# Regrouping the input loads of a one-token attention and GLU kernel: one load for wq, four heads of K per load, V in four, two, one and one heads

## The chip, the cores and the metric

The kernel runs on one core of a Trainium2 chip. The core has a matrix engine (TensorE, PE in the profile, with its weight loads as PEld), a vector engine (VectorE, DVE), a scalar engine (ScalarE, ACT), GpSimd (POOL) and SyncE (SP), which here only issues data transfers. Sixteen DMA engines move data between the off-chip memory and the on-chip memory. The metric is the device time of one execution in microseconds. Before the change it is 82.23 us, the median of five runs (82.16 to 82.81).

## The reference

One token `x` (512 values) goes through two branches, and a sigmoid gate mixes them. Branch A is attention over the last 4096 positions of a cache with 8 key/value heads and 32 query heads of 128 values. Branch B is a gated linear unit of width 1792.

```python
W = min(4096, max(256, Sk // 4))                 # 4096
q = (x @ wq) in 32 heads of 128
k = k_cache[:, :, Sk - W:, :]; v = v_cache[:, :, Sk - W:, :]   # each head serves 4 query heads
p = softmax(q @ k^T * Dh ** -0.5)
a = (p @ v) flattened @ wo
b = (sigmoid(x @ w_gate) * (x @ w_up)) @ w_down
g = sigmoid(sum(x * gate_w))
out = g * a + (1 - g) * b
```

All inputs are bfloat16. They come to 30.67 MB: wq and wo 4.19 MB each, the windows of K and V 8.39 MB each, w_gate, w_up and w_down 1.84 MB each. Each byte is used once.

## The kernel before, in words

**Loads.** All large inputs are loaded by one queue, SyncE's (`dq = nc.sync`), in the order of the program: wq in two halves (line 77), K in four loads of two heads (`kn`, line 86 through `load_blocks`, line 80), w_gate and w_up (lines 90 and 92), V in loads of two, two, two and one heads (`vv`, lines 102 and 104), half of w_down (105), V's last head (106), the rest of w_down (107), and wo in six pieces (112). The two short vectors `x` and `gate_w` come through ScalarE's queue (lines 70 and 71).

**Buffers.** K and V share the pool `blk`. It has four buffers, and each holds two heads: for each of the 128 partitions, 32 rows of 128 values of each head, 8 KB per head. V's first four-buffer round therefore goes where K was: the first V load waits until VectorE has read heads 0 and 1 of K, the second until it has read heads 2 and 3, and so on. wo uses wq's buffer (tag `big`). SyncE executes its instructions in order, so all that stands behind a waiting load waits too. A load also waits for the load that used its completion semaphore before, which is about eight loads earlier.

**Query.** TensorE computes q with x's four chunks as the stationary side and wq as the moving side: 32 matmuls of 512 columns in four blocks (line 160). ScalarE copies each block to on-chip memory (162), VectorE transposes it in 32 x 32 blocks (163), and eight small VectorE copies place it in a zeroed selection matrix `qbig` (172).

**Scores.** For each of the eight key heads VectorE transposes the head's K in 32 x 32 blocks of 4-byte elements (`kT`, line 180; four buffers), and eight matmuls accumulate scores for all heads in one PSUM tile (185). VectorE and ScalarE then form the softmax numerators (192 to 205) and VectorE transposes them (`eT`, 207).

**Branch B, values, output.** 32 matmuls make gate and up (215), VectorE and ScalarE the gated product and its transpose (221 to 231). The value matmuls (267) take eight per head and wait for the V load of their head. Heads are handled in two groups of four; each group ends with a ScalarE copy (272), eight small matmuls (277) and a VectorE multiplication (279). After the second group VectorE and TensorE bring the result into columns (283 to 287). `add_row` (248) accumulates w_down's and wo's products in one row: 28 matmuls for w_down and 64 for wo. The result is copied and stored in two halves (294 to 297).

The order on each engine is set by a scheduler of the framework, which moves instructions between the independent chains; the order of the loads on SyncE is the program's.

Of the kernel before, what the change touches and what calls it, by code (L numbers as in the profile page):

```python
# [12 lines left out]
BF16 = mybir.dt.bfloat16  # L13
# [4 lines left out]
def kernel(  # L18
# [16 lines left out]
    P = 128  # L35
    D = A_x.shape[-1]
    DC = D // P
    Hkv = A_k_cache.shape[1]
# [5 lines left out]
    KB = W // P  # L44
# [12 lines left out]

    const = ctx.enter_context(tc.tile_pool(name="const", bufs=1))
    big = ctx.enter_context(tc.tile_pool(name="big", bufs=1))
    blk = ctx.enter_context(tc.tile_pool(name="blk", bufs=4))  # L60
    w14 = ctx.enter_context(tc.tile_pool(name="w14", bufs=3))
    ktp = ctx.enter_context(tc.tile_pool(name="ktp", bufs=4))
    work = ctx.enter_context(tc.tile_pool(name="work", bufs=1))
# [9 lines left out]
    dq = nc.sync  # L73
    wq_sb = big.tile([P, DC, HQ * DH], BF16, name="wq_sb", tag="big")
    wq_v = A_wq.rearrange("(p c) n -> p c n", c=DC)
    for i in range(2):
        dq.dma_start(wq_sb[:, 2 * i:2 * i + 2, :], wq_v[:, 2 * i:2 * i + 2, :])  # L77

    def load_blocks(t, cache, g0, n, at=0):
        dq.dma_start(t[:, at:at + n, :, :],  # L80
                     cache[0, g0:g0 + n, SBASE:SBASE + W, :].rearrange("g (p kb) d -> p g kb d", kb=KB))

    kn = []
    for i in range(Hkv // 2):
        t = blk.tile([P, 2, KB, P], BF16, name="kn", tag="blk")
        load_blocks(t, A_k_cache, 2 * i, 2)
        kn += [t[:, 0], t[:, 1]]

    wg_sb = w14.tile([P, DC, F], BF16, name="wg_sb", tag="w14")
    dq.dma_start(wg_sb[:], B_w_gate.rearrange("(p c) f -> p c f", c=DC))  # L90
# [4 lines left out]
    wd_v = B_w_down.rearrange("(p j) n -> p j n", j=NJ)  # L95

    vv = []
    for i in range(Hkv // 2):
        t = blk.tile([P, 2, KB, P], BF16, name="vv", tag="blk")
        vv += [t[:, 0], t[:, 1]]  # L100
        if i < Hkv // 2 - 1:
            load_blocks(t, A_v_cache, 2 * i, 2)
        else:
            load_blocks(t, A_v_cache, 2 * i, 1)
            dq.dma_start(wd_sb[:, 0:NJ_A, :], wd_v[:, 0:NJ_A, :])
            load_blocks(t, A_v_cache, 2 * i + 1, 1, at=1)
            dq.dma_start(wd_sb[:, NJ_A:NJ, :], wd_v[:, NJ_A:NJ, :])

    wo_sb = big.tile([P, NC_O, N_OUT], BF16, name="wo_sb", tag="big")
# [218 lines left out]
```

## Time and profile before

| | |
|---|---|
| median of 5 runs | 82.23 us |
| profiled execution, its own time | 82.23 us |
| its span, first to last instruction | 80.2 us |
| TensorE busy | 51.2 us, 64% of the span |
| VectorE busy | 35.2 us, 44% |
| ScalarE busy | 9.0 us, 11% |
| queue of the loads | 30.67 MB, its packets fill 92.4% of 16 engines' span |
| transposes of K, line 180 | 8 of 2274 ns |
| score matmuls, line 185 | 64, busy 16.1 us |
| value matmuls, line 267 | 64, busy 12.7 us |

The span is what the profile covers; the time of a run also holds what lies before the first and after the last instruction. Busy time is a union of an engine's instructions. Matmuls are pipelined and overlap, so the mean duration of one is longer than the pace at which they go; where a pace is needed, it is read from a stretch of time and the number of matmuls that it holds. "DMA to landing" is the time from the issue of a load to its completion, with the wait in the queue. In rows by window the columns are the window, its length, busy time and number of instructions of PE, PEld, DVE, ACT and POOL, the granted TensorE clock, the DMA engines' busy share, and GB/s.

### The profile page before, as it was taken

Reading aid. Unit: us, or ns where it says so; the run is one execution under the profiler, and the core shown is the slowest. Engines: PE = TensorE matmul, PEld = TensorE weight load, DVE = VectorE, ACT = ScalarE, POOL = GpSimd, SP = SyncE. Lnnn points to the kernel's source line nnn. Section 1 sums busy time; section 2 is a strip of 40 time slices with the busy share of each in tenths; the row PEclk is TensorE's granted clock in tenths of the full one; section 3 lists DMA queues with packets and bytes.
Section 4 is the critical chain, followed back from the end, with each engine's and each line's share of the span. In section 5 each row is a group of like instructions: output and inputs, shape, how many; then the busy total and the mean of one; then the engine's idle time right before and its main releaser. Section 6 shows DMA issues by size and latency. Waiting matters only on the chain.

```text
span 80.2 us, 777 instructions
## 1 busy us (share of the span) xinstructions
PE 51.2 (64%) x313; PEld 23.2 (29%) x313; DVE 35.2 (44%) x43; ACT 9.0 (11%) x13; POOL 5.0 (6%) x10
## 2 busy tenths in 40 slices
PE   0010995999200499999997475958599656745560
PEld 0000531334000133444442233322533323533330
DVE  0006400052999999999923437999100000200020
ACT  2300000555500000000000080001100002000010
POOL 7970000000000000000000000000000000000000
PEclk9999999999995557999999999999955999999996
DMA  5699999999999999999999999999999999999400
GB/s 99 261 425 417 449 433 384 445 413 437 413 437 404 433 409 430 444 429 436 415 408 425 404 429 417 421 425 417 428 415 440 411 424 403 425 421 396 181 11 1
DMA packets 3930, 30.71 MB, mean 383 GB/s; under 512 B 340, under 2 KB 472, under 8 KB 984
## 3 DMA queue, kind: packets, MB, share of 16 engines
q1 hardware_dynamic: 3922, 30.67, 92.4%
q8 instruction: 2, 0.03, 0.2%
q10 hardware_dynamic: 6, 0.00, 0.0%
HBM read 30.67 MB, written 0.00 MB: 382 GB/s over the span
## 4 chain that ended last, share of the span: by engine, by line
DMA 65%; DVE 15%; PE 9%; issue 6%; ACT 1%; SPq 0%
DMA vv<-in_A_v_cache_dram 27%; DMA wo_sb<-in_A_wo_dram 23%; DMA wq_sb<-in_A_wq_dram 15%; DVE kT L180 11%; PE q_ps L160 7%; DVE qbig L172 2%; DVE qtT L163 2%; PE a_ps L248 2%; ACT q_sb L162 1%; DVE res L294 0%; SPq L77 0%
## 5 line engine op out<-in xcount | busy, mean ns | idle before, releaser
L185 PE MATMUL S_ps<-kT,qbig 128*128 128x512 bf16 x64 | 16.1, 414 | 6.6 <-DVE qbig L172 6.6
L180 DVE STREAM_TRANSPOSE kT<-kn 128x2048 f32<-128x2048 f32 x8 | 17.8, 2274 | 0.0
L267 PE MATMUL pv_ps<-vv,eT 128*16 128x512 bf16 (+1 forms) x64 | 12.7, 435 | 3.0 <-DMA vv<-in_A_v_cache_dram 3.0
L160 PE MATMUL q_ps<-wq_sb,xT 128*128 128x512 bf16 x32 | 11.1, 524 | 0.8 <-DMA wq_sb<-in_A_wq_dram 0.8
L185 PEld LDWEIGHTS <-qbig 128*128 128x128 bf16 x64 | 6.6, 104 | 16.1 <-DVE qbig L172 7.4
L267 PEld LDWEIGHTS <-eT 128*16 128x16 bf16 (+1 forms) x64 | 4.6, 99 | 10.0 <-issue 5.5
L163 DVE STREAM_TRANSPOSE qtT<-q_sb 128x512 f32<-128x512 f32 x4 | 2.8, 700 | 9.0 <-ACT q_sb L162 9.0
L248 PE MATMUL a_ps<-wo_sb,oY 128*1 128x256 bf16 x64 | 4.3, 272 | 3.1 <-DMA wo_sb<-in_A_wo_dram 3.1
L160 PEld LDWEIGHTS <-xT 128*128 128x128 bf16 x32 | 3.9, 126 | 7.5 <-issue 6.2
L279 DVE TENSOR_TENSOR oT<-o_ps,rb 128x16 bf16<-128x16 f32 x2 | 0.3, 175 | 12.4 <-PE o_ps L277 12.4
L162 ACT CAST q_sb<-q_ps 128x1024 bf16<-128x1024 f32 x4 | 4.0, 1012 | 8.7 <-PE q_ps L160 8.7
L248 PEld LDWEIGHTS <-oY 128*1 128x1 bf16 x64 | 2.8, 83 | 4.5 <-issue 3.7
L294 DVE CAST res<-a_ps 1x256 bf16<-1x256 f32 x1 | 0.4, 411 | 7.9 <-PE a_ps L248 7.9
L141 DVE TENSOR_TENSOR gpr<-xr 1x512 f32<-1x512 bf16 x1 | 0.7, 680 | 6.7 <-DMA xr<-in_gate_w_dram 6.7
L133 PE MATMUL xt_ps<-ident,xr 1*128 1x1 bf16 x4 | 0.3, 165 | 5.2 <-POOL ident L118 5.2
L126 POOL MEMSET qbig<- 128x4160 bf16 x1 | 3.6, 3564 | 0.0
L272 ACT COPY pv_sb<-pv_ps 128x512 f32<-128x512 f32 x2 | 1.2, 586 | 18.2 <-PE pv_ps L267 18.2
L277 PE MATMUL o_ps<-identf,pv_sb 128*128 128x16 f32 x16 | 2.1, 265 | 1.4 <-ACT pv_sb L272 1.4
L224 DVE RECIPROCAL sg<-sge 128x448 f32<-128x448 f32 x1 | 3.0, 2954 | 0.0
L202 ACT ACTIVATE nb<-mb_ps 128x1 f32<-128x1 f32 x1 | 0.2, 171 | 24.4 <-PE mb_ps L199 24.4
L277 PEld LDWEIGHTS o_ps<-identf,pv_sb 128*128 128x128 f32 x16 | 1.9, 191 | 2.4 <-ACT pv_sb L272 2.4
L192 DVE TENSOR_REDUCE pm<-S_ps 128x1 f32<-128x1024 f32 x1 | 1.2, 1225 | 2.7 <-PE S_ps L185 2.7
(49 smaller groups left out, 26.0 us busy)
## 6 DMA issues: line engine op xcount, KB each, us to landing
kn<-in_A_k_cache_dram SPq DMA_DIRECT2D x4, 2048.0 KB, 20.8
vv<-in_A_v_cache_dram SPq DMA_DIRECT2D x3, 2048.0 KB, 21.4
wq_sb<-in_A_wq_dram SPq DMA_DIRECT2D x2, 2048.0 KB, 9.6
wo_sb<-in_A_wo_dram SPq DMA_DIRECT2D x3, 1024.0 KB, 24.1
vv<-in_A_v_cache_dram SPq DMA_DIRECT2D x2, 1024.0 KB, 19.7
wg_sb<-in_B_w_gate_dram SPq DMA_DIRECT2D x1, 1792.0 KB
wu_sb<-in_B_w_up_dram SPq DMA_DIRECT2D x1, 1792.0 KB, 32.6
wd_sb<-in_B_w_down_dram SPq DMA_DIRECT2D x2, 896.0 KB, 21.5
```

The costliest lines, as they stand in the source:

```text
L126: nc.gpsimd.memset(qbig[:], 0.0)
L160: nc.tensor.matmul(q_ps[:, hb, :], lhsT=xT[:, c:c + 1].to_broadcast([P, P]), rhs=wq_sb[:, c, n0:n0 + 512], start=(c == 0), stop=(c == DC - 1))
L162: nc.scalar.copy(q_sb[:, k * 1024:(k + 1) * 1024], q_ps[:].rearrange("p a b -> p (a b)"))
L163: nc.vector.transpose(qtT[:].bitcast(F32)[:, k * 512:(k + 1) * 512], q_sb[:].bitcast(F32)[:, k * 512:(k + 1) * 512])
L172: nc.vector.tensor_copy(q_dst[rows, :, 32 * qd:32 * qd + REP, :, t], q_src[rows, :, :, :, 0, t])
L180: nc.vector.transpose(kT[:].bitcast(F32), kn[g].rearrange("p k d -> p (k d)").bitcast(F32))
L185: nc.tensor.matmul(S_ps[:, hb, :], lhsT=q_st[:, g, dhi, :, t], rhs=k_v[:, hb * 16:(hb + 1) * 16, dhi, :, t], start=(g == 0 and dhi == 0 an ...
L192: nc.vector.tensor_reduce(pm[:], S_f, axis=AX.X, op=ALU.max)
L224: nc.vector.reciprocal(sg[:], sge[:])
L248: nc.tensor.matmul(a_ps[32 * i:32 * i + 1, i, 0:HN], lhsT=lhsT, rhs=rhs[:, i * HN:(i + 1) * HN], start=start, stop=stop)
L267: nc.tensor.matmul(pv_ps[32 * gq:32 * gq + mm, :, :], lhsT=eT[:, g, 4 * m:4 * m + wj, :].rearrange("p k h -> p (k h)"), rhs=vv[g][:, 4 * m ...
L277: nc.tensor.matmul(o_ps[:], lhsT=pv_sb[:, j, :], rhs=sel_v[:, j, :, :], start=(j == 0), stop=(j == 3))
```

## The change

The pool `blk` gets two buffers of four heads in place of four buffers of two; the memory is the same. wq is loaded by one transfer. K is loaded by two transfers of four heads. V is loaded by one transfer of four heads into the first buffer, and into the second by transfers of two, one and one heads, with the halves of w_down between as before. Nothing else is edited.

```diff
-    blk = ctx.enter_context(tc.tile_pool(name="blk", bufs=4))
+    blk = ctx.enter_context(tc.tile_pool(name="blk", bufs=2))
...
-    for i in range(2):
-        dq.dma_start(wq_sb[:, 2 * i:2 * i + 2, :], wq_v[:, 2 * i:2 * i + 2, :])
+    dq.dma_start(wq_sb[:], wq_v)
...
-    for i in range(Hkv // 2):
-        t = blk.tile([P, 2, KB, P], BF16, name="kn", tag="blk")
-        load_blocks(t, A_k_cache, 2 * i, 2)
-        kn += [t[:, 0], t[:, 1]]
+    for i in range(2):
+        t = blk.tile([P, 4, KB, P], BF16, name="kn", tag="blk")
+        load_blocks(t, A_k_cache, 4 * i, 4)
+        kn += [t[:, j] for j in range(4)]
...
-    for i in range(Hkv // 2):
-        t = blk.tile([P, 2, KB, P], BF16, name="vv", tag="blk")
-        vv += [t[:, 0], t[:, 1]]
-        if i < Hkv // 2 - 1:
-            load_blocks(t, A_v_cache, 2 * i, 2)
+    for i in range(2):
+        t = blk.tile([P, 4, KB, P], BF16, name="vv", tag="blk")
+        vv += [t[:, j] for j in range(4)]
+        if i == 0:
+            load_blocks(t, A_v_cache, 0, 4)
         else:
-            load_blocks(t, A_v_cache, 2 * i, 1)
+            load_blocks(t, A_v_cache, 4, 2)
+            load_blocks(t, A_v_cache, 6, 1, at=2)
             dq.dma_start(wd_sb[:, 0:NJ_A, :], wd_v[:, 0:NJ_A, :])
-            load_blocks(t, A_v_cache, 2 * i + 1, 1, at=1)
+            load_blocks(t, A_v_cache, 7, 1, at=3)
             dq.dma_start(wd_sb[:, NJ_A:NJ, :], wd_v[:, NJ_A:NJ, :])
```

## The prediction

> **What bounds the kernel now.** I read the page's slices and queues first, then the chain that ended last, then SyncE's own instructions and waits, then the stages of the DMA stream.
>
> ```profile
> DMA  5699999999999999999999999999999999999400
> DMA packets 3930, 30.71 MB, mean 383 GB/s; under 512 B 340, under 2 KB 472, under 8 KB 984
> q1 hardware_dynamic: 3922, 30.67, 92.4%
> q8 instruction: 2, 0.03, 0.2%
> ```
>
> The DMA engines are full from the third slice (4 us) to the thirty-seventh (74 us). 92.4% of 80.2 us is 74.1 us of packets per engine: all 30.67 MB arrive through one queue without a hole. The chain, in order of time, ends so:
>
> ```profile
> 36.28 21.65 DMA vv<-in_A_v_cache_dram
> 57.92 0.02 issue
> 57.94 18.38 DMA wo_sb<-in_A_wo_dram
> 76.32 0.04 issue
> 76.36 1.25 PE a_ps L248 x16
> 77.61 0.40 DVE res L294
> ```
>
> From 36.3 us on the chain is load, load, sixteen matmuls, a copy. All arithmetic before that is behind the stream. So two questions decide: does the change shorten the stream, and does any engine become so late that the stream runs dry, or that work is left over when it ends?
>
> ```profile
> 1.64 2.21 SPq L80 DMA_DIRECT2D kn<-in_A_k_cache_dram  x4
> 25.67 15.34 SPq L80 DMA_DIRECT2D vv<-in_A_v_cache_dram  x4
> SPq L80 <- DVE kT L180: 21.2, 4, 7.6
> L180 DVE STREAM_TRANSPOSE kT<-kn x8: 2268/2268/2312, 20.6 to 38.4; 128x2048 f32<-128x2048 f32 x8
> DMA to landing us min/median/max: 16.3/20.8/25.2
> ```
>
> The first two are SyncE's timeline, the third its waits, the last two the instructions on the tile kn. V loads wait for VectorE's transposes, because they reuse K's buffers; the first is issued at 25.67. K loads landed at 1.64 + 16.3 = 17.9, then about 22.9 (2.11 + 20.8), then 27.95 (2.75 + 25.2): 5.0 us per 2 MB, with no gap between them. The transposes occupy VectorE nearly without a pause from 20.6 to 40.6.
>
> ```profile
> 8.00:13.00 5.00, 4.11 (x10) 1.69 (x11) 0.89 (x6) 0.17 (x1) 0.00 (x0) 1.00 0.99 424
> 14.00:32.00 18.00, 11.36 (x36) 4.09 (x35) 13.40 (x17) 4.05 (x4) 0.00 (x0) 0.81 1.02 425
> 33.00:40.50 7.50, 7.50 (x36) 3.31 (x34) 7.50 (x4) 0.00 (x0) 0.00 (x0) 1.00 1.01 428
> 42.00:57.00 15.00, 10.41 (x81) 4.63 (x80) 9.79 (x11) 2.51 (x5) 0.00 (x0) 1.00 1.01 419
> ```
>
> These are windows (last columns: TensorE clock, DMA share, GB/s): mostly wq, then K, then gate and up, then V. Packets of 16, 8, 14 and 8 KB run at 424, 425, 428 and 419 GB/s: the size of packets above 8 KB hardly matters.
>
> **Part 1, fewer and larger loads.** wq 2 loads become 1, K 4 become 2, V 5 become 4: four fewer. K and V keep their 8 KB packets, since one head's rows for a partition are 8 KB whatever the load holds. Only wq changes packets: a partition's four chunks lie together, so 32 KB in place of 2 x 16 KB. The trace's single packets, by size, have medians of 312 ns (8 KB), 540 (14 KB), 611 (16 KB) and 9 (the 4 B semaphore write that each engine makes per load). The straight line through 8 and 16 KB has 0.0365 ns per byte and 13 ns at zero, so an estimate for 32 KB is 13 + 1196 = 1209 ns. Per engine: wq 16 x 611 = 9.78 becomes 8 x 1209 = 9.67, a gain of 0.10; four semaphore writes 4 x 9 = 0.04. Sum -0.14 us.
>
> No row shows a 32 KB packet. Lower end: -0.10 as worked out. Upper end: the sixteen first packets of wq take 1.2 to 1.7 us, about 0.7 over 0.61; if this start-up grew with the packet, doubling it would add 0.7. Nearer rows deny growth: single 8 KB packets ahead of the kernel exceed their 0.31 by 0.13 to 0.24, the two 16 KB instruction fetches exceed 0.61 by 0.41 in the middle of traffic, so it looks like latency. If packets are cut back to 16 KB, 0. I take -0.10.
>
> **A rule weighed.** The Trainium skill's page "DMA: Bandwidth & Descriptors", section "Anatomy of one DMA — SWDGE (gpsimd) path", gives a DMA about 2.0 us fixed plus bytes / 436e3, measured on the other issue path. Paid in turn, a 2 MB K load would take 2.0 + 4.8 = 6.8 us, and four fewer loads would save 8 us: 74. The row says 5.0 us from landing to landing, which leaves room for 0.2 at most, and most of this is data at 425 GB/s (4.93). The fixed part is hidden under the next load's packets. I take the row: -0.04.
>
> **Part 2, q starts later.** Half of wq let 8 matmuls run in 8.64 to 12.23; the other 24 began at 13.06. Now all 32 begin when wq is whole, about 12.9. Ends of the q blocks, read from where ScalarE's copies start, are 14.94, 16.65, 18.90, 20.62: after the restart, eight matmuls in 3.59 us, eight in 2.25, eight in 1.72. So 32 take 3.59 + 2.25 + 2 x 1.72 = 9.3, to 22.2, 1.6 later. The page "TensorE: Matmul & The Clock Gate", section "Part 1: The HAM clock gate (the "warmup" mystery)", speaks against the change: lost early work is lost warm-up, some 3.4 us at half clock after an idle time. By the rule 8 cold matmuls (3.4) and 24 warm (24 x 0.216 = 5.2) end at 21.5. The row is 0.7 longer; I take it. The granted clock reads 1.00 here, but the 0.45 us per matmul in the row shows the slow start.
>
> **Part 3, K lands in fours.** Heads 0 to 3 now land when heads 2 and 3 did, 22.9 instead of 17.9; heads 4 to 7 at 32.9 as before. VectorE: the last q copy ends at 23.3, its transpose at 24.0, eight selection copies (1.76) at 25.8, then eight transposes at a pitch of 2.21: heads 0 to 3 done at 34.6, the eighth at 43.5, 2.9 later than 40.6. If two transposes go ahead of the copies, as now, the sums stay within 0.5.
>
> Score matmuls: start 28.0. TensorE has then idled 5.8 us, and will start slow as now (10 in 4.26 us at clock 0.54, the other 54 at 0.217 each). That needs 16.0, to 44.0, but the last head can only begin at 43.5: 43.5 + 8 x 0.217 = 45.2, 2.0 later than 43.2. From there to the transposed weights eT it is 5.5 us as now (43.23 to 48.74): 50.7.
>
> **Part 4, V's waits.** The first V load needs heads 0 to 3: issue at 34.6 instead of 25.7. Queued behind it on SyncE are all other V loads, wd and wo, and TensorE and the stream wait for those. The cover is wu: it lands at 8.90 + 32.6 = 41.5, and a first packet starts 1.0 after issue (0.74 to 1.74). The stream runs dry only if that V load is issued after about 40, so 5 us are spare. The second half needs head 7 (43.5); by then the first 4 MB keep the stream busy until about 51, so 7 us are spare. The loads of wd and wo keep their order; their waits on a load some eight earlier end later (wo's third on the first V load, 52.9), with 10 us of data still queued. SyncE's long issue of wg (4.96 us) stays harmless: nothing follows until 34.6. Cost 0.
>
> **Part 5, TensorE catches up.** Heads 0 to 3 start when the 4 MB V load lands, with heads 2 and 3 now: 52.9. 4 x 1.39 = 5.6 to 58.5, copy 0.65, eight small matmuls 1.06: 60.2. Heads 4 to 6 take 4.2 (64.4), half of wd 0.93 (65.3), head 7 1.9 (67.2), against 67.0 now. A stretch at half clock adds about 0.04 per matmul (16 in 3.44 against 16 in 2.78), 0.7 for one stretch. The slack at the end: after the o chain (69.36 now) TensorE needs 0.93 + 4 x 1.04 = 5.1 us, so it could start as late as 77.57 - 5.1 = 72.5: 3.1 us spare. Cost 0; without the cover each us is one us.
>
> **Sum.** 80.21 - 0.14 = 80.07 in the span; the profiled execution took 82.23, the median too, so 2.0 lie around it: **82.1 us**.
>
> **Rivals.**
> - TensorE becomes the bound (slower). Mechanism: half clock lasts through the score matmuls. From eT to the o chain TensorE needs 18.6 us less the wait for V, 16.7 of work, so it decides only when eT is later than 72.5 - 16.7 = 55.8, with half clock (0.427 each) beyond about 46. If it lasted throughout, 28.0 + 27.3 + 5.5 + 16.7 = 77.5, 5.0 past 72.5: up to 87; a typical case 83.5. For it: the record has 0.50 in the stage already. Against: it ended after 6.8 us. 0.06.
> - Start-up grows with wq's packet: 82.1 + 0.7 = 82.8. 0.07.
> - Instruction fetches collide (slower). Among the trace's single packets, the two instruction fetches at 41.90 and 66.35 each leave one engine about 1.5 us behind the other fifteen to the end; they hit different engines, and the last wo load completes on fourteen by 75.7, on two at 77.2. On one engine it would be 83.6. Nothing in the change steers that. 0.04.
> - Larger loads stream better (faster): wq, K and V (20.97 MB) at 428 instead of 421 is 0.8 us: 81.3. Against: 8 KB packets sit at 309 to 314 ns. 0.09.
> - The stream bounds as now: 0.74.
>
> **How the numbers follow.** 0.5% (0.41 us) is what a measurement can tell. Likeliest 82.1. The range 81.75 to 82.8 holds the stream's case and the start-up rival, and leaves out the two other slower ones and most of the faster one (0.18). Faster 0.09, same 0.74, slower 0.06 + 0.07 + 0.04 = 0.17.
>
> **What would show it.** DMA full to about 75 and wo's last landing near 77.1; first V issue near 34.6, ahead of wu's landing; q ending near 22, transposes near 43.5, the first value matmul near 53; 17 loads' worth of semaphore packets. Wrong if the DMA row has a hole near 41, if the last wo matmuls no longer wait for a DMA, or if wq lands past 13.5.

## The result and the profile after

The changed kernel takes 81.94 us, the median of 43 runs (81.64 to 82.34), against 82.20 for the kernel before (80 runs). The ratio of the two is 0.9954, with a 95% interval from 0.9943 to 0.9966. That is 0.26 us by the medians and 0.38 by the ratio, faster by about the 0.5% that was called the limit of what a measurement can tell. The prediction was 82.1 in a range of 81.75 to 82.8, with no change as the likeliest. An execution that took over 1.5% more than the fastest of its kernel counts as slow and is left out of the ratios, which below concerns one of four executions of the kernel with one buffer, four of twelve with 6 more matmuls and two of four with 24.

The page of the changed kernel, slices and queues:

```profile
span 80.1 us, 774 instructions
DMA  6869979999999999999999999999999999999400
DMA packets 3739, 30.71 MB, mean 383 GB/s; under 512 B 277, under 2 KB 409, under 8 KB 921
q1 hardware_dynamic: 3730, 30.67, 92.1%
q8 instruction: 2, 0.03, 0.2%
```

The stream is full as before, to the thirty-seventh slice, with no hole near 41 us (the first slices are uneven, since 32 KB packets are counted where they start). There are 192 packets fewer: 128 of wq and 64 semaphore writes. The span is 80.1 where it was 80.2.

The end of the chain, in order of time:

```profile
26.15 6.79 DVE kT L180 x4
...
43.84 13.93 DMA vv<-in_A_v_cache_dram
57.77 0.02 issue
57.79 18.35 DMA wo_sb<-in_A_wo_dram
76.14 0.04 issue
76.19 1.27 PE a_ps L248 x16
77.46 0.40 DVE res L294
```

It ends as before: load, load, sixteen matmuls, copy, 0.15 to 0.18 us earlier. The transposes of K now begin at 26.15, and V's second load leaves at 43.84, when the last is done.

SyncE's and VectorE's timelines and TensorE's, the lines that answer to the steps of the prediction:

```profile
35.07 9.66 SPq L79 DMA_DIRECT2D vv<-in_A_v_cache_dram  x3
26.15 17.66 DVE L180 STREAM_TRANSPOSE kT<-kn 128x2048 f32<-128x2048 f32 x8
49.09 2.95 DVE L224 RECIPROCAL sg<-sge 128x448 f32<-128x448 f32 x1
51.96 1.19 DVE L207 STREAM_TRANSPOSE eT<-e_sb 128x1024 bf16<-128x1024 bf16 x1
13.04 9.38 PE L160 MATMUL q_ps<-wq_sb,xT 128*128 128x512 bf16 x32 [3.04 <-DMA wq_sb<-in_A_wq_dram]
55.34 0.61 PE L237 MATMUL rb_ps<-lsel,ones_f 128*128 128x32 f32 x2 [6.86 <-DVE lsel L235]
55.88 5.89 PE L267 MATMUL pv_ps<-vv,eT 128*32 128x512 bf16 x32
74.61 1.04 PE L248 MATMUL a_ps<-wo_sb,oY 128*1 128x256 bf16 x16 [1.26 <-DMA wo_sb<-in_A_wo_dram]
76.19 1.23 PE L248 MATMUL a_ps<-wo_sb,oY 128*1 128x256 bf16 x16 [0.54 <-DMA wo_sb<-in_A_wo_dram]
```

All 32 query matmuls wait for the whole of wq and take 9.38 us. V's first load leaves at 35.07, well ahead of the landing of w_up at 41.44. The value matmuls start at 55.88, and nevertheless TensorE waits for wo in the end: 1.26 and 0.54 us.

**Where the gain is.** Each execution has a time and a span (the spans to 0.1 us), and the two can be averaged separately. For the kernel before, the spans of the 68 executions beside the first four experiments are on record, for the changed one those of 44 executions of the result.

| mean over the executions | before | after | difference |
|---|---|---|---|
| span | 80.25 | 80.13 | -0.12 |
| of it: spans up to 80.3 | 80.06 (48 of 68) | 80.11 (42 of 44) | +0.05 |
| time less span | 2.04 | 1.80 | -0.24 |
| time | 82.29 | 81.93 | -0.37 |

So two thirds of the gain lie outside the span, and the rest comes from something that was rare afterwards: 20 of 68 executions of the kernel before have a span of 80.5 to 81.0 us, and only 2 of 44 of the changed kernel reach 80.5. The ordinary executions have not become shorter. The two columns come from two comparisons, but each of these alone says the same: beside the same 68 executions the changed kernel has a mean span of 80.10 and 1.79 outside it, and in the result's own comparison 25 of 80 executions of the kernel before take 82.47 us or more, where the slowest of 43 of the changed one takes 82.34. These two facts are what the experiments had to explain, and neither was in the prediction.

### The profile page after: what moved, and what is told of

Same layout as the page of the kernel before. It is cut to its first block, busy times and chain, and to the rows that moved or that the text cites. A ratio compares the mean times of both kernels' runs of the same rounds, so it can differ in the third digit from the quotient of the medians.

```text
span 80.1 us, 774 instructions
## 1 busy us (share of the span) xinstructions
PE 47.3 (59%) x313; PEld 22.5 (28%) x313; DVE 35.1 (44%) x43; ACT 8.8 (11%) x13; POOL 5.0 (6%) x10
## 4 chain that ended last, share of the span: by engine, by line
DMA 56%; DVE 21%; PE 13%; issue 5%; ACT 1%; DVEq 0%
DMA wo_sb<-in_A_wo_dram 23%; DMA vv<-in_A_v_cache_dram 17%; DVE kT L180 17%; DMA wq_sb<-in_A_wq_dram 15%; PE q_ps L160 12%; DVE qbig L172 2%; PE a_ps L248 2%; ACT q_sb L162 1%; DVE qtT L163 1%; DVE res L294 0%; DVEq L180 0%; DVEq L172 0%
## 5 line engine op out<-in xcount | busy, mean ns | idle before, releaser
L160 PE MATMUL q_ps<-wq_sb,xT 128*128 128x512 bf16 x32 | 9.4, 465 | 3.0 <-DMA wq_sb<-in_A_wq_dram 3.0
L267 PE MATMUL pv_ps<-vv,eT 128*16 128x512 bf16 (+1 forms) x64 | 10.8, 416 | 0.0
L237 PE MATMUL rb_ps<-lsel,ones_f 128*128 128x32 f32 x2 | 0.6, 398 | 6.9 <-DVE lsel L235 6.9
L221 ACT ACTIVATE sge<-gu_ps 128x448 f32<-128x448 f32 x1 | 0.5, 544 | 24.6 <-PE gu_ps L215 24.6
L144 PE MATMUL z_ps<-gsum,ones_f 1*128 1x1 f32 x2 | 0.6, 356 | 4.0 <-DVE gsum L142 4.0
```

Of the source, the lines that this page charges most:

```text
L160: nc.tensor.matmul(q_ps[:, hb, :], lhsT=xT[:, c:c + 1].to_broadcast([P, P]), rhs=wq_sb[:, c, n0:n0 + 512], start=(c == 0), stop=(c == DC - 1))
L267: nc.tensor.matmul(pv_ps[32 * gq:32 * gq + mm, :, :], lhsT=eT[:, g, 4 * m:4 * m + wj, :].rearrange("p k h -> p (k h)"), rhs=vv[g][:, 4 * m ...
```

## The experiments

The theory at the start (A) was the prediction's own: wq's larger packets shorten the stream. The rival (B): the gain belongs to K and V in fours. When the first runs had shown the gap between time and span, two theories were added for it, S (it follows the length of SyncE's program) and V (it follows VectorE's program or the form of the K and V loads), and TensorE's clock for the long spans.

### One part of the change at a time

wq alone in one load, on the kernel before:

```diff
-    for i in range(2):
-        dq.dma_start(wq_sb[:, 2 * i:2 * i + 2, :], wq_v[:, 2 * i:2 * i + 2, :])
+    dq.dma_start(wq_sb[:], wq_v)
```

> The kernel before with wq in one load, K and V left as they were. Theory A (the gain is in wq's packets: 32 KB instead of 16 KB): nearly the whole gain is here, 0.15 to 0.25 us under the kernel before. Rival B (the gain is in the fewer K and V loads and what they reorder): 0.05 us or less.

K and V alone in fours, that is the changed kernel with wq in two loads:

```diff
-    dq.dma_start(wq_sb[:], wq_v)
+    for i in range(2):
+        dq.dma_start(wq_sb[:, 2 * i:2 * i + 2, :], wq_v[:, 2 * i:2 * i + 2, :])
```

> The changed kernel with wq in two loads again, K and V grouped. Theory A: K's and V's packets stay at 8 KB, three fewer semaphore writes per engine, so 0.03 us under the kernel before, not to be told from no change. Rival B: about 0.2 us under it.

The changed kernel with wq in four loads:

```diff
-    dq.dma_start(wq_sb[:], wq_v)
+    for i in range(4):
+        dq.dma_start(wq_sb[:, i:i + 1, :], wq_v[:, i:i + 1, :])
```

> The changed kernel with wq in four loads, each of one 8 KB chunk per partition. Theory A: per engine 32 packets of 0.312 instead of 8 of 1.212, 9.98 against 9.70, and three more semaphore writes: 0.3 us over the changed kernel, which is level with the kernel before. Rival B: level with the changed kernel, 0.2 us under the one before.

And the changed kernel beside them.

> The changed kernel itself beside the three, on the same chip: 0.2 to 0.3 us under the kernel before. It is the yardstick: under theory A the first of the three equals it, under rival B the second.

| kernel | ratio to before | 95% interval | mean span | spans over 80.3 | time less span |
|---|---|---|---|---|---|
| before | 1 | | 80.25 | 20 of 68 | 2.04 |
| wq in one | 0.999 | 0.9965 to 1.0015 | 80.21 | 9 of 22 | 2.06 |
| K, V in fours | 0.9971 | 0.9946 to 0.9995 | 80.29 | 5 of 22 | 1.80 |
| fours, wq in four | 0.9982 | 0.9959 to 1.0005 | 80.31 | 13 of 22 | 1.81 |
| both (changed kernel) | 0.9945 | 0.9921 to 0.997 | 80.10 | 0 of 15 | 1.79 |

Theory A falls: wq alone brings nothing that can be told from no change, where 0.15 to 0.25 us was expected. Rival B is right about the place and wrong about the reason. K and V in fours bring 0.24 us, all of it in the time outside the span; their spans are no shorter. The last column takes two values, 2.04 to 2.06 with pairs and 1.79 to 1.81 with fours, and in each kernel single executions stay within 0.1 of it. With K and V in fours, wq in one load goes with a mean span 0.19 shorter (80.29 to 80.10). That too is no shorter stream: the spans up to 80.3 average 80.12 and 80.10, and what is missing is the long ones (5 of 22, 0 of 15).

The packets themselves did what the prediction said. In the trace 32 KB packets have a median of 1213 ns (1209 was estimated), and their total per engine, with the slow first one, fell from 10.53 to 10.30 us. But a load is complete when the slowest of the sixteen engines is, and that one did not gain. The first piece with wq in the chains of the kernel before, of the changed kernel and of K and V in fours (the first and the third with wq's second half):

```profile
1.17 11.85 DMA wq_sb<-in_A_wq_dram
0.74 12.26 DMA wq_sb<-in_A_wq_dram
1.17 11.73 DMA wq_sb<-in_A_wq_dram
```

That is 13.02, 13.00 and 12.90. Over all profiled executions wq is complete at 12.89 to 13.21 in one load, at 12.89 to 13.02 in two and at 12.90 and 13.02 in four; averaged over the sixteen engines it is 12.63 to 12.74 in one and 12.73 to 12.78 in two.

### What the time outside the span follows

The kernel before with K and V in pairs, and three loads fewer elsewhere:

```diff
-    for i in range(2):
-        dq.dma_start(wq_sb[:, 2 * i:2 * i + 2, :], wq_v[:, 2 * i:2 * i + 2, :])
+    dq.dma_start(wq_sb[:], wq_v)
...
-    WO_SPLIT = (0, 8, 16, 24, 29, 31, 32)
+    WO_SPLIT = (0, 16, 24, 29, 31, 32)
...
-            dq.dma_start(wd_sb[:, 0:NJ_A, :], wd_v[:, 0:NJ_A, :])
+            dq.dma_start(wd_sb[:], wd_v)
...
-            dq.dma_start(wd_sb[:, NJ_A:NJ, :], wd_v[:, NJ_A:NJ, :])
```

> The kernel before with K and V as they were (pairs of heads, four buffers), and three loads fewer elsewhere: wq in one, w_down in one, wo's first two pieces in one; 18 input loads on SyncE as against 21. The question is the time outside the span, 2.0 to 2.1 us in the kernel before and with wq alone in one load, 1.7 to 1.8 in every kernel with K and V in fours. Theory S (it follows the length of SyncE's program): 1.8. Theory V (it follows VectorE's program or the K and V form): 2.0 to 2.1. In the span the larger packets are worth at most 0.3 us.

The changed kernel with five loads more:

```diff
-    dq.dma_start(wq_sb[:], wq_v)
+    for i in range(4):
+        dq.dma_start(wq_sb[:, i:i + 1, :], wq_v[:, i:i + 1, :])
...
-    dq.dma_start(wg_sb[:], B_w_gate.rearrange("(p c) f -> p c f", c=DC))
+    for i in range(2):
+        dq.dma_start(wg_sb[:, 2 * i:2 * i + 2, :], B_w_gate.rearrange("(p c) f -> p c f", c=DC)[:, 2 * i:2 * i + 2, :])
...
```

w_up is loaded alike.

> The changed kernel with more loads elsewhere: wq in four, w_gate and w_up in two each; 22 input loads on SyncE as against 17. Theory S: 2.0 to 2.1 us outside the span. Theory V: 1.8. In the span 0.1 to 0.4 us more than the changed kernel, from packets of 8 and 7 KB.

Measured outside the span: 2.07 us with pairs and 18 loads, 1.81 with fours and 22 loads, where the kernel before beside them has 2.06. Theory S falls: it is not the number of loads. Theory V stands, and its two halves are not told apart: in the trace VectorE's program has 54 instructions in each kernel with pairs and 57 in each with fours, waits included, so it changes with the form of the loads. Its mere length is not the reason, since the loads-only kernel below, in fours with 7 VectorE instructions, lies at 1.76. What in pairs and four buffers costs 0.25 us before the first or after the last profiled instruction was not found. In the span the 0.1 to 0.4 us expected of the five loads more did not show: its spans up to 80.3 average 80.09. (Times: pairs with fewer loads 82.07, ratio 0.9984, interval 0.9965 to 1.0002; fours with more loads 81.98, ratio 0.9986, interval 0.9962 to 1.001.)

### The long spans

The profiled execution of "fours, wq in four" has a span of 80.4, between the two groups of the kernel before, and shows a possible cause. Its chain's last pieces, and windows of 3 us at the end of it (columns: TensorE, its weight loads, VectorE, ScalarE, GpSimd, clock, DMA share, GB/s):

```profile
52.81 21.78 DMA wo_sb<-in_A_wo_dram
74.59 0.04 issue
74.64 3.32 PE a_ps L249 x32
77.96 0.40 DVE res L295
```

```profile
72.00:75.00 3.00, 1.40 (x20) 0.91 (x21) 0.00 (x0) 0.00 (x0) 0.00 (x0) 0.84 0.95 377
75.00:78.00 3.00, 2.92 (x32) 1.75 (x26) 0.05 (x1) 0.02 (x1) 0.00 (x0) 0.59 0.09 32
```

TensorE's granted clock fell to 0.59 in the last window (cut finer, it is 0.50 from 74.06 to 77.47 and 1.00 on both sides), and TensorE was busy for 2.92 of 3 us: 32 matmuls in 3.32 us, where the kernel before does its last 16 in 1.25 after a pause. From wo's last landing (77.11) to the issue of the output it took 1.26 us instead of 0.78. So the suspicion: in the long spans the clock has dropped while TensorE waited between wo's pieces. The test gives the kernel before more to do there:

```diff
         add_row(oY[:, c:c + 1], wo_sb[:, c, :], False, c == NC_O - 1)
+        if c < 24 and c % 8 > 4:
+            nc.tensor.matmul(fill_ps[:], lhsT=oY[:, c:c + 1], rhs=wo_sb[:, c, :], start=True, stop=True)
```

> The kernel before with 9 more matmuls of 512 columns, three at the end of each of wo's first three pieces, into a scratch row; the output does not use them. In the kernel before 20 of 68 executions have a span of 80.5 to 81.0 instead of 79.9 to 80.3. Theory (in these TensorE's clock has fallen to half while it waits between the pieces of wo, and the last matmuls are slow): with less idle time there the long spans become rare, under 1 in 10, and the others stay. Rival (the long spans come from the loads, or from the instruction fetches): 3 in 10 as before.

None of its 22 executions has a span over 80.2; beside it the kernel before has 21 of 69 over 80.3. The mean of the ordinary spans is the same, 79.98 and 80.01. The time is 82.02, ratio 0.9971 (0.9953 to 0.999), by more work. Windows of the kernel before and of this one:

```profile
72.00:75.00 3.00, 1.26 (x21) 0.87 (x22) 0.00 (x0) 0.00 (x0) 0.00 (x0) 1.00 0.98 390
75.00:78.00 3.00, 2.03 (x32) 1.20 (x26) 0.40 (x1) 0.36 (x1) 0.00 (x0) 1.00 0.09 33
```

```profile
72.00:75.00 3.00, 3.00 (x35) 1.85 (x33) 0.00 (x0) 0.00 (x0) 0.00 (x0) 0.87 0.96 381
75.00:78.00 3.00, 2.28 (x29) 1.25 (x24) 0.41 (x1) 0.36 (x1) 0.00 (x0) 1.00 0.07 26
```

The kernel before is at full clock in the end of this execution, but it works only 1.26 us of 72 to 75. The filled kernel works all three, even comes from half clock (0.56 in 69 to 72, 0.60 in 72 to 73), and is at full clock when wo's last piece arrives. So work in the pauses removes the long spans. That the clock is what stands between the two is seen in the one long execution that was profiled, and no long execution of the kernel before was profiled. But each execution's mean clock is on record, and it goes with the span: of 41 long executions (over 80.3 us) of the kernel before, 39 have a clock of 0.915, 0.916 or 0.937, of 96 ordinary ones 16. By 2 x (1 - clock) x span these are 13.7 and 10.2 us of half clock, four and three whole stretches of 3.41 us as the one above. In most of the long executions, then, no stretch is cut off by the end of the span; in the profiled ordinary one a stretch begins at 79.0 and is cut off.

The Trainium skill's page "TensorE: Matmul & The Clock Gate", section "Part 1: The HAM clock gate (the "warmup" mystery)", has the clock fall after an idle window of about 3.4 us and return after a busy one, with windows that run freely. The length agrees with the trace (74.06 to 77.47), and windows that run freely would explain why the same program falls on either side from execution to execution. That the window has to be idle does not agree: before the fall TensorE was busy 1.41 us of 70.65 to 74.06. In the kernel before it kept full clock after 1.83 us of 72.16 to 75.57. How much work keeps the clock is not settled by these runs: in the filled kernel it fell at 69.39 after 2.23 us of 65.98 to 69.39, most of them value matmuls.

How many matmuls TensorE does from 72 to 75 us in the one profiled execution of each kernel, beside its long spans:

| kernel | matmuls in 72 to 75 us | spans over 80.3 |
|---|---|---|
| fours, wq in four | 20 | 13 of 22 |
| before | 21 | 20 of 68, 21 of 69 |
| K, V in fours | 24 | 5 of 22 |
| fours with more loads | 24 | 9 of 22 |
| wq in one | 28 | 9 of 22 |
| changed kernel | 34 and 41 | 2 of 44, 0 of 15 |
| pairs with fewer loads | 34 | 0 of 22 |
| before, filled | 35 | 0 of 22 |
| larger loads at the end, below | 44 | 5 of 16 |

Roughly, all but the last row fit: where TensorE's work comes closer together there, long spans are rare, and the pairs with fewer loads lose them without one matmul more. For the changed kernel this is an argument, not a test, and the last row, with as much work there and 5 long spans, speaks against its being the whole reason. That was not settled.

### What the prediction called free

V's wait, moved to the last head of K:

```diff
-    blk = ctx.enter_context(tc.tile_pool(name="blk", bufs=2))
+    blk = ctx.enter_context(tc.tile_pool(name="blk", bufs=1))
...
+    t = blk.tile([P, 8, KB, P], BF16, name="kn", tag="blk")
+    kn += [t[:, j] for j in range(8)]
     for i in range(2):
-        t = blk.tile([P, 4, KB, P], BF16, name="kn", tag="blk")
-        load_blocks(t, A_k_cache, 4 * i, 4)
-        kn += [t[:, j] for j in range(4)]
+        load_blocks(t, A_k_cache, 4 * i, 4, at=4 * i)
...
```

V's buffer and loads follow alike.

> The changed kernel with K and V in one buffer of eight heads; the loads keep their sizes. The first V load now waits for the last head of K, 43.8 us instead of 35.1. Theory (V's wait is free only while wg and wu are still arriving, to about 41.4, and a load's first packet starts 1.0 us after issue): the stream stands still for about 3.4 us, and the time is 3 to 3.5 us over the changed kernel. Rival (enough is queued, or later work has room): no more than 0.5 us.

86.86 us, ratio 1.0541 (1.0485 to 1.0598): 4.9 us over the changed kernel, more than expected. SyncE's timeline and windows of 1 us, of the longest of four executions (span 86.1; the others 84.6 to 85.1):

```profile
44.05 1.44 SPq L79 DMA_DIRECT2D vv<-in_A_v_cache_dram  x3
40.00:41.00 1.00, 1.00 (x7) 0.40 (x6) 1.00 (x1) 0.00 (x0) 0.00 (x0) 1.00 0.48 201
41.00:42.00 1.00, 0.71 (x4) 0.29 (x3) 1.00 (x2) 0.00 (x0) 0.00 (x0) 1.00 0.00 0
44.00:45.00 1.00, 0.92 (x5) 0.44 (x5) 0.02 (x1) 0.00 (x0) 0.00 (x0) 1.00 0.00 0
45.00:46.00 1.00, 1.00 (x9) 0.34 (x11) 0.00 (x0) 0.00 (x0) 0.00 (x0) 1.00 0.74 254
46.00:47.00 1.00, 1.00 (x18) 0.46 (x17) 0.98 (x1) 0.00 (x0) 0.00 (x0) 1.00 0.90 360
```

The stream does not end at w_up's landing, 41.4: the first of the sixteen engines is done with w_up at 40.5 and the last at 41.0, and the landing is seen 0.4 us after that. V's load leaves at 44.05, its first packet starts at 45.1, and it takes until 47 for the full rate. Missing against 415 GB/s from 40 to 48 are 5.0 us. (What this execution takes beyond that is at its end, where wo's last 32 matmuls take 3.42 us at half clock.) The cover is real, and it ends for a V load issued after about 39.4, which is 40.5 less the 1.05 us from issue to first packet; the prediction said 40. With the issue at 35.07 some 4.3 us are spare.

TensorE's spare time, with more value matmuls at the first head (n = 6 and 24):

```diff
-            for m in range(KB // 4):
+            for m in [0] * (n if g == 0 else 0) + list(range(KB // 4)):
```

> The changed kernel with 6 more value matmuls of the same form ahead of the first head; their product is overwritten. About 1.1 us more TensorE work after the softmax. Theory (TensorE waits 1.8 us in total for wo's last pieces, 1.26 and 0.54, so it has 1.8 us to spare): no change. Rival (TensorE's late start already sets the end): 1 us slower.

> The changed kernel with 24 more value matmuls ahead of the first head, about 4.4 us more TensorE work. Theory: 1.8 us are covered, so 2 to 3 us slower than the changed kernel. If the load stream gave more cover than the two waits show: less than 1 us.

With 6 the median is 82.23 us (12 executions, ratio 0.9987, interval 0.9953 to 1.0021). But seven spans are 79.8 to 80.5 as in the changed kernel and five are 81.0 to 81.9. The profiled one is among the five. The end of its chain, and of the kernel with 24:

```profile
72.11 0.18 PE oY_ps L285
72.28 6.06 PE a_ps L248 x78
78.35 0.40 DVE res L294
```

```profile
75.56 0.18 PE oY_ps L285
75.73 4.39 PE a_ps L248 x78
80.13 0.40 DVE res L294
```

No DMA stands at the end of either: TensorE sets it. In the first, 78 matmuls take 6.06 us at a clock of 0.62 from 72 to 75; in the second 4.39 at full clock. So 1.8 us to spare hold at full clock, and half clock on these matmuls uses up 1.7 of them. With 24 the spans are 82.8 to 84.9 (85.85 us, ratio 1.0474, interval 1.0398 to 1.055). The profiled execution, at full clock to the end, is 2.7 us longer than the changed kernel, as expected; the median is 3.9 and the longest span 4.8 over it, and what these lost was not profiled.

### The stream by itself

All loads of the changed kernel; all computation is left out, so V's loads wait for no transpose, and the first leaves at 23.02:

> All loads of the changed kernel except the two short vectors' use, and no computation: the output is a piece of wo. No TensorE program is left, so nothing fetches its instructions during the stream. Theory (the two fetches leave two engines 1.4 us behind, and these set the end): all sixteen engines complete wo's last load within 0.5 us, near 75.6 us, and the time is 1.3 us + 0.3 us of last matmuls = 1.6 us under the changed kernel, 80.3. Rival (the lag is a property of two engines or of the loads): the lag stays and the time is 0.3 us under it, 81.6.

80.15 us, ratio 0.9748 (0.9711 to 0.9785), 1.8 us under the changed kernel. Its queues, and windows of it and of the changed kernel:

```profile
q1 hardware_dynamic: 3730, 30.67, 94.2%
q10 hardware_dynamic: 6, 0.00, 0.0%
```

```profile
74.00:75.00 1.00, 0.00 (x0) 0.00 (x0) 1.00 0.90 327
75.00:76.00 1.00, 0.17 (x1) 0.00 (x0) 1.00 0.04 12
76.00:77.00 1.00, 0.11 (x1) 0.00 (x0) 1.00 0.00 1
```

```profile
75.00:76.00 1.00, 0.65 (x12) 0.37 (x9) 0.00 (x0) 0.00 (x0) 0.00 (x0) 1.00 0.14 52
76.00:77.00 1.00, 0.81 (x14) 0.55 (x14) 0.00 (x0) 0.00 (x0) 0.00 (x0) 1.00 0.08 29
```

Without instructions to fetch (the queue of instruction packets is gone from the page), all sixteen engines have completed wo's last piece by 75.8. In the changed kernel fourteen are done by 75.7, and two, as many as there are 16 KB fetches (at 45.2 and 69.0), at 77.0 and 77.1. The last window is those two: a share of 0.08 is 1.3 engines of sixteen. The kernel with one buffer confirms that each fetch delays one engine: one of its fetches, at 42.9, falls into the stream's standstill, and only one engine is late there, at 82.4, with the other fifteen done by 80.8. Fetching instructions costs the changed kernel 1.3 us at the end. The rest of the 1.8 us is the last matmuls (0.78 us from landing to output issue against 0.33).

### Larger loads at the end

The changed kernel with w_down in one load and wo in five, the edits of the pairs kernel above:

> The changed kernel with w_down in one load and wo's first two pieces in one. Eight packets less per engine at each place, 13 ns each, 0.2 us less stream, if the packet's fixed part counts at the end of the stream; the span falls from 80.1 to 79.9, the time to 81.7. If only the slowest engine's place among the sixteen counts: level with the changed kernel.

82.04 us, ratio 0.9965 (0.9938 to 0.9992), level with the changed kernel. In the profiled execution wo's last piece landed at 76.84 instead of 77.10, as its packets promise, and the ordinary spans average 80.06 against 80.10; but 5 of 16 spans are long, and the gain is gone in them. A version of this with TensorE filled between wo's pieces was not run.

## Why the prediction was right, and where its sum was not

- **What bounds the kernel**: right. The stream is full to about 75 us and wo's last landing is at 77.10 (about 77.1 was said). The loads-only kernel confirms it, at 80.15.
- **Part 1, packets**: right in size per packet (1213 ns against 1209), wrong in what it buys. The -0.14 was summed as the mean of sixteen engines. The slowest engine decides, and it is done with wq no earlier in one load (12.89 to 13.21) than in two or four (12.89 to 13.02). The term should have been 0 for wq. The profiled pair shows 0.16 less at the end, but the ordinary spans of many executions do not (80.06 and 80.11).
- **The rule weighed, 2 us per load**: the row was right. Four loads fewer did not save 8 us, and kernels of 17 to 22 loads lie within 0.3 us.
- **The sum's last line**: this failed. "2.0 lie around it" was taken as a constant, and it became 1.8. This is 0.24 of the gain of 0.37, and the profile before could not show it. That 82.1 lies so near is in part luck: the 0.14 us that the sum took off did not come, and what came is in two places that it had at nothing.
- **Part 2, q**: 22.2 was said, 22.42 measured (13.04 + 9.38).
- **Part 3**: V's first issue 34.6 said, 35.07 measured; transposes done 43.5 said, 43.81 measured.
- **Part 4, V's wait**: free, as said. Its limit is nearer than said, 39.4 instead of 40, because the first engine runs out of packets 0.9 us before the landing.
- **Part 5, TensorE**: right in the outcome, wrong by the way. The value matmuls start at 55.88, not 52.9. The step that failed is "from there to eT it is 5.5 us as now": the framework's scheduler put the gate's reciprocal (2.95 us) ahead of eT, which came at 51.96 to 53.15 instead of 50.7, and the matmul for the row sums waited for VectorE until 55.3. TensorE's spare time shrank from 3.1 to 1.8 us.
- **The rival of the half clock**: its mechanism is real and was put in the wrong place. Through the scores it cost nothing. On wo's matmuls it is the likely cause of the 0.65 us (80.7 against 80.06) that 3 of 10 executions of the kernel before take longer, which the prediction did not see since the one profiled execution had none. That these got rarer is the second part of the gain.
- **The rival of the start-up**: it falls. wq's first packets of 32 KB take 1.2 to 2.1 us, on average 0.6 over the 1.21 of the others, where those of 16 KB (1.0 to 1.7 us; the prediction read 1.2 to 1.7) had 0.7 over 0.61.

## What to carry to other kernels

Here one queue was always full, and merging its loads did not shorten the stream: read the packets, not the loads, and then the slowest engine, not the mean. Where TensorE waits for the last pieces of a stream, its clock can fall just before it is needed, so a few matmuls more in the pauses can make a kernel steadier, as 9 of them did here. Compare time and span separately over many executions: a change of 0.3% can lie outside everything that the profile shows.

## What the runs showed of the hardware

- A 16 KB instruction fetch leaves its DMA engine about 1.5 us behind, for the rest of a full stream: it takes 1.0 to 1.1 us, and the 8 KB data packet after it 0.77 to 0.86 us instead of 0.31. The Trainium skill's page "Runtime: NRT & Kernel Launch", section "Instruction fetch mechanics", calls fetches hidden by the pace of issue. In TensorE's timeline no matmul waits for a fetch, which agrees; for the load stream fetches are not hidden (1.3 us at the end).
- A 32 KB packet takes 1213 ns and four of 8 KB 1248, nearly the same rate.
- A load that starts into an empty queue needed about 1 us to the first packet and about 2 more to the full rate; a completion was seen 0.4 us after the last packet (w_up in the kernel with one buffer, 40.98 and 41.41).
- Half clock came in stretches of 3.41 us or whole multiples, also after such a stretch in which TensorE had been busy for 1.41 us (with wo) or 2.23 us (mostly value matmuls).
- Time less span differs by 0.25 us between two forms of the same loads, and is constant within 0.1 us for each. Its cause stays open.
